# Constants as PE filler, later loads of x8-15, and half an output tile behind the state matrix M

## The chip, the cores and the metric

One core of one Trainium2 chip. The metric is the device time of one execution in microseconds; "span" is what the profile of one execution shows on the core, about 1.7 to 2 us less than that time. The engines are named as in the profile: PE multiplies matrices, PEld loads its weights, DVE, ACT and POOL compute on vectors, SP issues DMAs. The "pitch" is the time from the start of one matmul to the start of the next. "The clock opens" means that the pitch of matmuls with 128 columns falls from 107 to 56 ns; where a time is given for it, it is the start of the trace's first clock record, which the printed views do not show. All runs here carry the state "fast".

## The reference

A layernorm `xn` of x (2048 tokens, 640 features) feeds two branches, and the output is the sum of x and both:

```
xn = layernorm(x)
A: q,k,v = xn @ wqkv (32 heads of 20); phi(t) = where(t > 0, t + 1, exp(t)) + 1e-6
   num = phi(q) @ (phi(k)^T v);  den = phi(q) . sum_s phi(k) + 1e-6;  A = (num / den) @ wo
B: gelu(xn @ w1 + b1) @ w2 + b2          (hidden size 1536)
out = x + A + B
```

Only the start (layernorm, first matmuls with W1) and the join of both branches (the state matrix M, the denominators, the product with W2) matter here.

## The kernel before

x is cut into 16 tiles of 128 tokens. Every tile is normalised on DVE with help of POOL. Tiles 0 to 2 are transposed by PE, tiles 3 to 15 by DMA, issued from SP in order with the loads. A planner turns declared reads and writes of "resources" into semaphore waits; a wait that an earlier instruction of the same engine implied already is left out.

The head, with matmuls on zeros ("filler") that keep PE busy while x arrives, and the loads:

```python
dma_x(0, 1); dma_x(1, 1); dma_w1(0); dma_w1(1); dma_x(2, 1); dma_x(3, 1)   # one line each
dma_w1(2); dma_x(4, 2); dma_w1(3); dma_x(6, 2); dma_x(8, 4)
Pl.ins(v, lambda e: e.memset(warm[:].bitcast(FP32), 0.0), writes=[r_warm])
# ... (cut)
def filler(n):
    b = take(1)
    Pl.ins(pe, [lambda e: e.matmul(bank(b), warm[:, 0:P], warm[:], start=True, stop=True)
                for _ in range(n)], reads=[r_warm], writes=[B_[b]])
def ln_half(t, h):
    s = t % 4
    Pl.ins(v, lambda e: e.bn_stats(stats[:, s, 6*h:6*h+6], x_in[:, t, h*HW:(h+1)*HW]),
           reads=r_x[t], writes=[r_stats[s]])          # one resource for both halves
def ln_aggr(t):
    s = t % 4
    if t < 2:
        Pl.ins(v, lambda e: e.tensor_single_scalar(stats[:, s, 2:3], stats[:, s, 2:3], D * EPS, ALU.add), ...)
    Pl.ins(v, lambda e: e.bn_aggr(aggr[:, s, :], stats[:, s, :]), ...)
    # ... (cut) from tile 2 on POOL adds eps; then POOL: rstd = var ** -0.5
filler(9)
ln_half(0, 0); ln_half(0, 1); ln_aggr(0); ln_half(1, 0); ln_half(1, 1); ln_norm(0)
# ... (cut) transposes of tile 0, b1, filler(1), tile 1
def ln_rest():
    for t in range(4, NT):
        if t + 1 < NT:
            ln_half(t + 1, 0); ln_half(t + 1, 1)       # statistics of t+1 stand before
        ln_norm(t)                                     # the normalisation of t
        if t + 1 < NT: ln_aggr(t + 1)
        xnT_dma(t)                                     # DMA transpose of tile t
        if t == 7: dma_x(12, 4)
```

PE then runs h = W1^T xn^T for tiles 0 to 3 one by one, (4,5), (6,7), (8 to 11), (12 to 15). Much later:

```python
out_mm(0, 0, JT, b0, HALF[:1], [b0])          # W2, tile 0, first half of the columns
den_mm(b0 + 1)                                # denominators, into bank b0+1
m_step([0, 1, DT-1, 2, 3], ahead[1:] + ahead[1:3], lambda: den_eps(b0 + 1))  # M; den_eps after the 2nd
den_rec(); ...; scale_pq(0)
out_mm(0, 0, JT, b0, HALF[1:], [b0 + 1])      # W2, tile 0, second half: wants bank b0+1
for t in range(1, 4):
    out_mm(t, 0, JT, ahead[t], HALF, [ahead[t], ahead[t] + 1])
```

Of the kernel before, what the change touches and what calls it, by code (L numbers as in the profile page):

```python
# [5 lines left out]
ALU = AluOpType  # L6
ACT = mybir.ActivationFunctionType
P = 128
FP32 = mybir.dt.float32
BF16 = mybir.dt.bfloat16  # L10
# [102 lines left out]
def bass_parallel_sum__linear_attn_block__dense_activation_gelu__prompt_kernel(  # L113
    nc: bass.Bass, A_x, A_wqkv, A_wo, B_x, B_w1, B_b1, B_w2, B_b2, out):
    Batch, S, D = A_x.shape
# [7 lines left out]
    JT = F // P  # L123
# [11 lines left out]
    EPS = 1e-5  # L135

    Pl = Planner(nc)
    R_ = Pl.res

    with contextlib.ExitStack() as es:  # L140
        sb = lambda *a, **k: es.enter_context(nc.sbuf_tensor(*a, **k))
# [25 lines left out]
        b1c = sb("b1c", [P, JT], FP32)  # L167
        b2bc = sb("b2bc", [P, D], BF16)
        ident = sb("ident", [P, P], BF16)
        onesm = sb("onesm", [P, P], BF16)  # L170
        hmask = sb("hmask", [P, 3, H], BF16)
        maskKV = sb("maskKV", [P, 2, WD], BF16)
        ZB = sb("ZB", [P, DT, H], BF16)
        warm = sb("warm", [P, 512], BF16)
        stats = sb("stats", [P, 4, 12], FP32)
        aggr = sb("aggr", [P, 4, 2], FP32)
        veps = sb("veps", [P, 4], FP32)
# [10 lines left out]
        B_ = [R_("bank%d" % i) for i in range(8)]  # L188
        ring = [0]

        def take(n):
            b = ring[0]
            if n == 2 and b % 2:
                b += 1
            b %= 8
            ring[0] = (b + n) % 8
            return b

        def bank(b, lo=0, hi=512):
            return ps[:, b * 512 + lo: b * 512 + hi]  # L200
# [4 lines left out]
        def halves(ap):  # L205
            return ap.rearrange("p (a n) -> p a n", a=2)

        r_x = [[R_("x%d" % t)] for t in range(NT)]
# [7 lines left out]
        r_Wq, r_Wv, r_W2 = R_("Wq"), R_("Wv"), R_("W2")  # L216
        r_Wo = [R_("Wo%d" % w) for w in range(NW)]
        r_b1tmp, r_b1c, r_b2 = R_("b1tmp"), R_("b1c"), R_("b2")
        r_ident, r_small, r_ones, r_masks, r_hmask, r_warm = (
            R_("ident"), R_("small"), R_("ones"), R_("masks"), R_("hmask"), R_("warm"))  # L220
        r_stats = [R_("stats%d" % i) for i in range(4)]
        r_aggr = [R_("aggr%d" % i) for i in range(4)]
        r_veps = [R_("veps%d" % i) for i in range(4)]
        r_rstd = [R_("rstd%d" % i) for i in range(NT)]
# [19 lines left out]
        g = "gpsimd"  # L244
        v = "vector"
        s_ = "scalar"
        pe = "tensor"

        def dma(eng, dst, src, writes, reads=()):
            Pl.ins(eng, lambda e: e.dma_start(dst, src), reads=reads, writes=writes, dma=True)  # L250
# [4 lines left out]
        def dma_x(t, n):  # L255
            dma("sync", x_in[:, t:t + n, :], xv[t * P:(t + n) * P, :].rearrange("(t p) d -> p t d", p=P),
                sum(r_x[t:t + n], []))

        def dma_w1(i):
# [10 lines left out]
        dma_x(4, 2)  # L270
        dma_w1(3)
        dma_x(6, 2)
        dma_x(8, 4)

        Pl.ins(v, lambda e: e.memset(warm[:].bitcast(FP32), 0.0), writes=[r_warm])
        Pl.ins(g, lambda e: e.memset(onesm[:], 1.0), writes=[r_ones])
        Pl.ins(g, lambda e: e.memset(mhalf[:], -0.5), writes=[r_small])
        Pl.ins(g, lambda e: e.memset(ident[:], 0.0), writes=[r_ident])
# [3 lines left out]
               reads=[r_ident], writes=[r_ident])  # L282
# [19 lines left out]
            for _ in range(min(n, len(mask_jobs))):  # L302
                mask_jobs.pop(0)()

        def filler(n):
            b = take(1)
            Pl.ins(pe, [lambda e: e.matmul(bank(b), warm[:, 0:P], warm[:], start=True, stop=True)
                        for _ in range(n)], reads=[r_warm], writes=[B_[b]])

        def b1_step():  # L310
            b = take(1)
# [21 lines left out]
        def ln_half(t, h):  # L333
            s = t % 4
            Pl.ins(v, lambda e: e.bn_stats(stats[:, s, 6 * h:6 * h + 6], x_in[:, t, h * HW:(h + 1) * HW]),  # L335
                   reads=r_x[t], writes=[r_stats[s]])

        def ln_aggr(t):
            s = t % 4
            if t < 2:  # L340
                Pl.ins(v, lambda e: e.tensor_single_scalar(stats[:, s, 2:3], stats[:, s, 2:3], D * EPS, ALU.add),
                       reads=[r_stats[s]], writes=[r_stats[s]])
            Pl.ins(v, lambda e: e.bn_aggr(aggr[:, s, :], stats[:, s, :]),
                   reads=[r_stats[s]], writes=[r_aggr[s]])
            if t < 2:
                var, r_var = aggr[:, s, 1:2], r_aggr[s]
            else:
                var, r_var = veps[:, s:s + 1], r_veps[s]
                Pl.ins(g, lambda e: e.tensor_single_scalar(var, aggr[:, s, 1:2], EPS, ALU.add),
                       reads=[r_aggr[s]], writes=[r_var])  # L350
            Pl.ins(g, lambda e: e.tensor_tensor(out=rstd[:, t:t + 1], in0=var, in1=mhalf[:], op=ALU.pow),
                   reads=[r_var, r_small], writes=[r_rstd[t]])
# [30 lines left out]
        def xnT_dma(t):  # L383
            dma_t("sync", xnT[:, :, t * P:(t + 1) * P], xn_tm[:, t, :], r_xnT[t], reads=r_xn[t])

        def h_unit(t0, n, jb):
# [8 lines left out]
                HG[:, jb, tok], bank(b, 0, w), ACT.Gelu_apprx_tanh, bias=b1c[:, jb:jb + 1]),  # L395
                reads=[B_[b], r_b1c], writes=[r_HG[t][jb] for t in range(t0, t0 + n)])

        Pl.ins(s_, lambda e: e.activation(b1c[:, 0:1], warm[:, 0:1], ACT.Gelu_apprx_tanh),
               reads=[r_warm], writes=[r_b1c])

        dma(s_, b1tmp[:], B_b1.rearrange("(a p) -> a p", p=P), [r_b1tmp])
        filler(9)
        ln_half(0, 0)
        ln_half(0, 1)
        ln_aggr(0)
# [3 lines left out]
        b = take(2)  # L409
        transp2(0, b, b + 1)  # L410
        ln_aggr(1)
        copy2(0, b, b + 1)
        b1_step()
        filler(1)
        ln_norm(1)

        h_list = lambda t, n, lo, hi: [(t, n, jb) for jb in range(lo, hi)]
# [6 lines left out]
# [3 lines that stand above are left out]
                    ln_half(t + 1, 0)  # L427
                    ln_half(t + 1, 1)
                ln_norm(t)
                if t + 1 < NT:  # L430
                    ln_aggr(t + 1)
                xnT_dma(t)
                if t == 7:
                    dma_x(12, 4)

        for u in plan:
            if u == "T1":
                b = take(2)
# [8 lines left out]
            elif u == "T2":  # L447
                b = transp(2)
# [36 lines left out]
        for t in range(NT):  # L485
            b = take(2)
# [20 lines left out]
        for k in range(DT):  # L507
            for i in range(DT):
                Pl.ins(g, lambda e, k=k, i=i: e.tensor_copy(plain(Wqkv[:, k, D:2 * D], i), parts(Wqkv[:, k, 0:D], i)),  # L509
                       reads=[r_Wq], writes=[r_Wk, r_WqP])  # L510
# [87 lines left out]
        def m_step(js, bs, after):  # L598
            for n, (j, b) in enumerate(zip(js, bs)):
                for h in range(2):  # L600
                    fns, reads = [], []
                    for a in range(2 if j == DT - 1 else 1):
                        for q in range(4):
                            if j == DT - 1:
                                w, i, last = 2 * q + a, 2, a == 1
                            else:
                                w, i, last = 4 * (j // 2) + q, j % 2, True
                            lhsT = KVP[i][:, w, :]
                            reads += [r_KVP[i], r_Wo[w]]
                            fns.append(lambda e, lhsT=lhsT, w=w, q=q, h=h, b=b, a=a, last=last: e.matmul(  # L610
                                bank(b + h, 0, HW)[32 * q:32 * q + 32, :], lhsT, Wo[:, w, h * HW:(h + 1) * HW],
                                start=(a == 0), stop=last))
                    Pl.ins(pe, fns, reads=reads, writes=[B_[b + h]])
                    m_copy(j, b, h)
                if n == 1:
                    after()

        def den_mm(b):
# [13 lines left out]
        def scale_pq(c):  # L632
            cc = slice(c * CW, (c + 1) * CW)
            for r, (lo, n) in enumerate(((0, 2), (2, 2), (4, 1))):
                Pl.ins(v, lambda e, r=r, lo=lo, n=n: e.tensor_tensor(
                    out=PQ[:, lo:lo + n, cc], in0=PQ[:, lo:lo + n, cc],
                    in1=rsp[:, c, r:r + 1, :].broadcast_to((P, n, CW)), op=ALU.mult),
                    reads=[r_rsp[c][r]] + r_PQ[c][lo:lo + n], writes=r_PQ[c][lo:lo + n])
# [26 lines left out]
        ahead = [(b0 + 2 * i) % 8 for i in range(4)]  # L665

        def out_mm(t, lo, hi, b, w0, w1):
            tok = slice(t * P, (t + 1) * P)
            seq = [(HG[:, jb, tok], W2[:, jb, :], [r_HG[t][jb], r_W2]) for jb in range(JT)]
            seq += [(PQ[:, j, tok], Msb[:, j, :], [r_PQ[t // CH][j]] + r_M[j]) for j in range(DT)]  # L670
            n = len(seq)
            for i in range(lo, hi):
                Pl.ins(pe, [(lambda e, i=i, x=x, bb=bb: e.matmul(  # L673
                    bank(bb, 0, x[1] - x[0]), seq[i][0], seq[i][1][:, x[0]:x[1]],
                    start=(i == 0), stop=(i == n - 1))) for x, bb in zip(w0, w1)],
                    reads=seq[i][2], writes=[B_[bb] for bb in w1], mark=(i in (JT - 1, n - 1)))

        NS = JT + DT
        HALF = [(0, HW), (HW, D)]
# [13 lines left out]
        for c in range(NC):  # L693
            spread(c)
        scale_pq(0)
        out_mm(0, 0, JT, b0, HALF[1:], [b0 + 1])
        for t in range(1, 4):
            b = ahead[t]
            out_mm(t, 0, JT, b, HALF, [b, b + 1])
        for t, b in enumerate(ahead):  # L700
            xb(t)
            out_mm(t, JT, NS, b, HALF, [b, b + 1])
            out_done(t, b)
            if t == 1:
                scale_pq(1)
        for t in range(4, NT - 1):
            b = ahead[t % 4]
# [5 lines left out]
        t = NT - 1  # L713
# [3 lines left out]
        for i, (lo, hi) in enumerate([(0, 320), (320, 512), (512, 640)]):  # L717
            b = take(1)
            r_o = R_("ol%d" % i)
            out_mm(t, 0, NS, b, [(lo, hi)], [b])  # L720
            s = t % 2
            Pl.ins(v, lambda e, lo=lo, hi=hi, b=b: e.tensor_tensor(  # L722
                out=out_sb[:, s, lo:hi], in0=bank(b, 0, hi - lo), in1=x_res[:, t, lo:hi], op=ALU.add),
                reads=[B_[b], r_xb[t]], writes=[r_o] + ([r_out[s]] if i == 0 else []))
# [40 lines left out]
```

## Time and profile before

| | before |
|---|---|
| time, median of 3 | 208.29 us |
| span of the profiled run | 206.39 us |
| first matmul of h | 6.92 us |
| from there to the last matmul group of M | 124.01 us |
| that group to the next matmul | 0.54 us |
| last matmul's end to end of span | 2.45 us |

The rows below the span are start times from the trace and differences of them.

The page of the kernel before, busy time of each engine and the chain of waits:

```profile
PE 201.6 (98%) x1599; PEld 137.6 (67%) x1605; DVE 111.5 (54%) x230; ACT 73.6 (36%) x148; POOL 33.9 (16%) x83
...
PE 95%; DVE 2%; DMA 1%; issue 1%; ACT 0%
```

PE is the bound; a gain has to come from the few places where it idles. Its head, from the timeline of before (start, duration, engine, line, operation, and in brackets the idle time before it):

```profile
1.26 4.02 PE L307 MATMUL ps<-warm 128*128 128x512 bf16 x9 [1.26 <-DVE warm L275]
...
4.17 0.15 DVE L341 TENSOR_SCALAR stats<-stats 128x1 f32<-128x1 f32 x1
...
5.79 0.66 PE L322 MATMUL ps<-ident,xn_tm 128*128 128x128 bf16 x5 [0.51 <-DVE xn_tm L363]
...
6.92 1.00 PE L390 MATMUL ps<-xnT,W 128*128 128x128 bf16 x15
```

The stall after M, from the timeline of before. The addition to the denominators (den_sb) must read its bank before PE may write the second half of tile 0 there:

```profile
130.72 0.68 DVE L626 TENSOR_SCALAR den_sb<-ps 128x512 f32<-128x512 f32 x1
...
131.46 0.31 PE L673 MATMUL ps<-W,HG 128*128 128x320 bf16 x1 [0.24 <-DVE den_sb L626]
```

### The profile page before, as it was taken

The numbers are of one execution on the slowest core, as the hardware profiler recorded it, in microseconds if no ns is written. First come the engines' busy times: TensorE is split into PE (matmuls) and PEld (weight loads), VectorE is DVE, ScalarE is ACT, GpSimd is POOL, SyncE is SP. The second block draws the span as 40 slices with busy tenths as digits, with TensorE's granted clock in tenths as the row PEclk, the third lists the DMA queues.
The fourth block names the chain that finished last, engine by engine and source line by source line (L and its number), as shares of the span: only waits on it lengthen the run. The fifth ranks groups of instructions, "written<-read, shape, count | busy, mean of one in ns | idle before, by whom it ended". The sixth has DMA issues, their size and how long they took to land.

```text
span 206.4 us, 3983 instructions
## 1 busy us (share of the span) xinstructions
PE 201.6 (98%) x1599; PEld 137.6 (67%) x1605; DVE 111.5 (54%) x230; ACT 73.6 (36%) x148; POOL 33.9 (16%) x83
## 2 busy tenths in 40 slices
PE   7899999999999999999999999999999999999995
PEld 2799987444457777777746445677777777777774
DVE  4798674000007888999358888833954322523322
ACT  2699887666676555111153554300000000000000
POOL 2245436400000001999000200000000000000000
PEclk9999999999999999999999999999999999999999
DMA  5996675899500000000000001978611010001011
GB/s 144 350 296 109 168 121 118 272 320 376 188 0 0 3 0 0 3 0 0 0 3 0 2 3 22 370 170 170 150 67 63 32 34 33 32 33 35 32 47 52
DMA packets 24827, 19.70 MB, mean 95 GB/s; under 512 B 9960, under 2 KB 24808, under 8 KB 24808
## 3 DMA queue, kind: packets, MB, share of 16 engines
q1 hardware_dynamic: 23056, 17.86, 29.9%
q10 hardware_dynamic: 1752, 1.58, 4.1%
q8 instruction: 13, 0.21, 0.5%
q14 instruction: 6, 0.05, 0.1%
HBM read 13.11 MB, written 2.62 MB: 76 GB/s over the span
## 4 chain that ended last, share of the span: by engine, by line
PE 95%; DVE 2%; DMA 1%; issue 1%; ACT 0%
PE ps L673 36%; PE ps L390 25%; PE ps L515 11%; PE ps L490 11%; PE ps L556 10%; DMA xPK<-in_A_x_dram 1%; DVE stats L335 1%; PE ps L566 1%; PE ps L620 1%; DVE Msb L595 0%; PE ps L322 0%; DVE den_sb L626 0%; PE ps L610 0%; DVE W L722 0%; DVE xn_tm L363 0%
## 5 line engine op out<-in xcount | busy, mean ns | idle before, releaser
L673 PE MATMUL ps<-W,HG 128*128 128x320 bf16 (+2 forms) x396 | 54.8, 295 | 0.2 <-DVE den_sb L626 0.2
L390 PE MATMUL ps<-xnT,W 128*128 128x128 bf16 (+2 forms) x477 | 52.7, 272 | 0.2
L673 PEld LDWEIGHTS ps<-W,HG 128*128 128x128 bf16 x396 | 38.1, 98 | 14.8 <-DVE den_sb L626 0.5
L390 PEld LDWEIGHTS ps<-xnT,W 128*128 128x128 bf16 x480 | 36.9, 98 | 15.6 <-issue 0.3
L394 ACT ACTIVATE HG<-ps,b1c 128x128 bf16<-128x128 f32 (+2 forms) x96 | 41.5, 475 | 12.1 <-PE ps L390 10.5
L684 DVE TENSOR_TENSOR W<-ps,xnT 128x640 bf16<-128x640 f32 x15 | 12.4, 825 | 35.8 <-PE ps L673 35.4
L478 ACT ACTIVATE ek<-ps 128x512 bf16<-128x512 f32 (+1 forms) x36 | 23.2, 645 | 20.4 <-PE ps L556 10.7
L479 DVE TENSOR_SCALAR ek<-ek 128x512 bf16<-128x512 bf16 (+1 forms) x36 | 11.0, 304 | 35.0 <-ACT ek L478 33.8
L673 PE MATMUL ps<-Msb,PQ 128*128 128x320 bf16 (+2 forms) x165 | 24.2, 295 | 0.0
L490 PE MATMUL ps<-Wqkv,xnT 128*128 128x320 bf16 x160 | 21.9, 299 | 0.0
L515 PE MATMUL ps<-xPK,xn_tm 128*128 128x320 bf16 x160 | 21.9, 299 | 0.0
L556 PE MATMUL ps<-xnT,Wqkv 128*128 128x512 bf16 x97 | 21.4, 379 | 0.2
L673 PEld LDWEIGHTS ps<-Msb,PQ 128*128 128x128 bf16 x165 | 15.9, 98 | 5.9
L490 PEld LDWEIGHTS ps<-Wqkv,xnT 128*128 128x128 bf16 x160 | 15.7, 98 | 6.2
L515 PEld LDWEIGHTS ps<-xPK,xn_tm 128*128 128x128 bf16 x160 | 15.7, 98 | 6.1
L509 POOL COPY Wqkv<-Wqkv 128x128 bf16<-128x128 bf16 x25 | 15.1, 603 | 22.9 <-PE ps L490 21.4
L335 DVE BATCH_NORM_STATS2 stats<-xPK 128x6 f32<-128x320 bf16 x32 | 15.2, 474 | 4.6 <-DMA xPK<-in_A_x_dram 4.1
L556 PEld LDWEIGHTS ps<-xnT,Wqkv 128*128 128x128 bf16 x100 | 9.7, 98 | 11.4
L481 DVE SCALAR_TENSOR_TENSOR PQ<-ps,ek 128x512 bf16<-128x512 f32 x20 | 13.8, 691 | 2.1
L481 DVE SCALAR_TENSOR_TENSOR xPK<-ps,ek 128x640 bf16<-128x640 f32 x16 | 13.2, 824 | 1.7
L527 DVE TENSOR_TENSOR Msb<-Msb,xPK 128x640 f32<-128x640 f32 x14 | 11.6, 825 | 0.5
L519 ACT ACTIVATE W<-ps 128x640 bf16<-128x640 f32 x5 | 3.5, 704 | 18.2 <-PE ps L515 18.2
(60 smaller groups left out, 82.6 us busy)
## 6 DMA issues: line engine op xcount, KB each, us to landing
xnT<-in_A_x_dram SPq DMA_DIRECT2D x4, 640.0 KB, 6.2
Wqkv<-in_A_wqkv_dram SPq DMA_DIRECT2D x3, 800.0 KB, 6.9
out_dram<-W SPq DMA_DIRECT2D x15, 160.0 KB, 1.8
W<-in_B_w_dram SPq DMA_DIRECT2D x4, 480.0 KB, 6.1
W<-in_B_w_dram SPq DMA_DIRECT2D x1, 1920.0 KB, 14.5
xn_tm<-rden ACTq DMA_DIRECT2D x12, 128.0 KB, 3.4
xPK<-in_A_x_dram SPq DMA_DIRECT2D x2, 640.0 KB, 7.2
Wo<-in_A_wo_dram SPq DMA_DIRECT2D x8, 160.0 KB, 8.4
```

The source lines that it names most:

```text
L335: Pl.ins(v, lambda e: e.bn_stats(stats[:, s, 6 * h:6 * h + 6], x_in[:, t, h * HW:(h + 1) * HW]), reads=r_x[t], writes=[r_stats[s]])
L390: Pl.ins(pe, [(lambda e, k=k: e.matmul(bank(b, 0, w), W1[:, k, jb * P:(jb + 1) * P], xnT[:, k, tok], start=(k == 0), stop=(k == DT - 1))) ...
L394: Pl.ins(s_, lambda e: e.activation(HG[:, jb, tok], bank(b, 0, w), ACT.Gelu_apprx_tanh, bias=b1c[:, jb:jb + 1]), reads=[B_[b], r_b1c], wri ...
L478: Pl.ins(s_, lambda e: e.activation(e2, src, ACT.Exp), reads=br, writes=[r_ek[s]])
L481: Pl.ins(v, lambda e: e.scalar_tensor_tensor(out=d2, in0=src, scalar=0.0, in1=e2, op0=ALU.max, op1=ALU.add), reads=br + [r_ek[s]], writes= ...
L490: fns.append(lambda e, k=k, h=h, b=b, t=t: e.matmul(bank(b + h, 0, HW), xnT[:, k, t * P:(t + 1) * P], Wqkv[:, k, D + h * HW:D + (h + 1) * ...
L509: Pl.ins(g, lambda e, k=k, i=i: e.tensor_copy(plain(Wqkv[:, k, D:2 * D], i), parts(Wqkv[:, k, 0:D], i)), reads=[r_Wq], writes=[r_Wk, r_WqP])
L515: Pl.ins(pe, [(lambda e, t=t, h=h, b=b, f=f, i=i: e.matmul(bank(b + h, 0, HW), xn_tm[:, t, f * P:(f + 1) * P], PK[:, t, h * HW:(h + 1) * H ...
L527: Pl.ins(v, lambda e, t=t: e.tensor_tensor(out=zsum, in0=zsum, in1=PK[:, t, :], op=ALU.add), reads=[r_PK[t], r_zsum], writes=[r_zsum])
L556: Pl.ins(pe, [(lambda e, k=k, j=j, b=b: e.matmul(bank(b), Wqkv[:, k, D + j * P:D + (j + 1) * P], xnT[:, k, cc], start=(k == 0), stop=(k == ...
L673: Pl.ins(pe, [(lambda e, i=i, x=x, bb=bb: e.matmul(bank(bb, 0, x[1] - x[0]), seq[i][0], seq[i][1][:, x[0]:x[1]], start=(i == 0), stop=(i = ...
L684: Pl.ins(v, lambda e: e.tensor_tensor(out=halves(out_sb[:, s, :]), in0=pair(b), in1=halves(x_res[:, t, :]), op=ALU.add), reads=B_[b:b + 2] ...
```

## The change

Its intent: keep PE busy from its first moment, so that its clock rises early; take the small addition off DVE's path in the head; keep the DMA transposes of tiles 3 to 5 clear of the big load of x8-11 in front of them; fill the stall after M.

```diff
-        dma_x(8, 4)
-        Pl.ins(v, lambda e: e.memset(warm[:].bitcast(FP32), 0.0), writes=[r_warm])
+        def filler(n, w=512):
+            Pl.ins(pe, [lambda e: e.matmul(bank(b, 0, w), nc.const_aps.tensor(1.0, [P, P], BF16),
+                                           nc.const_aps.tensor(1.0, [P, w], BF16), ...) ...], writes=[B_[b]])
-        r_stats = [R_("stats%d" % i) for i in range(4)]
+        r_stats = [[R_("stats%d_%d" % (i, h)) for h in range(2)] for i in range(4)]
@@ ln_half
-                   reads=r_x[t], writes=[r_stats[s]])
+                   reads=r_x[t], writes=[r_stats[s][h]])
+            if t < 2 and h == 0:
+                Pl.ins(g, lambda e: e.tensor_single_scalar(stats[:, s, 2:3], ..., D * EPS, ALU.add), ...)
@@ ln_aggr: the addition on DVE goes; reads=r_stats[s] (both halves)
@@ head
-        filler(9)
+        filler(10)
+        filler(6, P)
-        filler(1)
+        filler(3, P)
@@ ln_rest
-                if t == 7:
+                if t == 5:
+                    dma_x(8, 4)
                     dma_x(12, 4)
@@ m_step
-                if n == 1:
+                if n == 2:
                     after()
@@ after M
         scale_pq(0)
+        out_mm(3, 0, JT, ahead[3], HALF[:1], [ahead[3]])
         out_mm(0, 0, JT, b0, HALF[1:], [b0 + 1])
-        for t in range(1, 4):
+        for t in range(1, 3):
             ...
+        out_mm(3, 0, JT, ahead[3], HALF[1:], [ahead[3] + 1])
```

(Cut. ACT's first activation also reads a constant instead of `warm`, so it no longer waits for DVE.)

More of the change, by code (lines that the diff above doesn't have):

```diff
@@ L173, in bass_parallel_sum__linear_attn_block__dense_activation_gelu__prompt_kernel @@
         ZB = sb("ZB", [P, DT, H], BF16)
-        warm = sb("warm", [P, 512], BF16)
         stats = sb("stats", [P, 4, 12], FP32)
@@ L218, in bass_parallel_sum__linear_attn_block__dense_activation_gelu__prompt_kernel @@
         r_b1tmp, r_b1c, r_b2 = R_("b1tmp"), R_("b1c"), R_("b2")
-        r_ident, r_small, r_ones, r_masks, r_hmask, r_warm = (
-            R_("ident"), R_("small"), R_("ones"), R_("masks"), R_("hmask"), R_("warm"))
-        r_stats = [R_("stats%d" % i) for i in range(4)]
+        r_ident, r_small, r_ones, r_masks, r_hmask = (
+            R_("ident"), R_("small"), R_("ones"), R_("masks"), R_("hmask"))
+        r_stats = [[R_("stats%d_%d" % (i, h)) for h in range(2)] for i in range(4)]
         r_aggr = [R_("aggr%d" % i) for i in range(4)]
@@ L303, in run_masks @@
                 mask_jobs.pop(0)()
-        def filler(n):
+        def filler(n, w=512):
             b = take(1)
-            Pl.ins(pe, [lambda e: e.matmul(bank(b), warm[:, 0:P], warm[:], start=True, stop=True)
-                        for _ in range(n)], reads=[r_warm], writes=[B_[b]])
+            Pl.ins(pe, [lambda e: e.matmul(bank(b, 0, w), nc.const_aps.tensor(1.0, [P, P], BF16),
+                                           nc.const_aps.tensor(1.0, [P, w], BF16), start=True, stop=True)
+                        for _ in range(n)], writes=[B_[b]])
         def b1_step():
@@ L335, in ln_half @@
             Pl.ins(v, lambda e: e.bn_stats(stats[:, s, 6 * h:6 * h + 6], x_in[:, t, h * HW:(h + 1) * HW]),
-                   reads=r_x[t], writes=[r_stats[s]])
+                   reads=r_x[t], writes=[r_stats[s][h]])
+            if t < 2 and h == 0:
+                Pl.ins(g, lambda e: e.tensor_single_scalar(stats[:, s, 2:3], stats[:, s, 2:3], D * EPS, ALU.add),
+                       reads=[r_stats[s][0]], writes=[r_stats[s][0]])
         def ln_aggr(t):
             s = t % 4
-            if t < 2:
-                Pl.ins(v, lambda e: e.tensor_single_scalar(stats[:, s, 2:3], stats[:, s, 2:3], D * EPS, ALU.add),
-                       reads=[r_stats[s]], writes=[r_stats[s]])
             Pl.ins(v, lambda e: e.bn_aggr(aggr[:, s, :], stats[:, s, :]),
-                   reads=[r_stats[s]], writes=[r_aggr[s]])
+                   reads=r_stats[s], writes=[r_aggr[s]])
             if t < 2:
@@ L396, in h_unit @@
                 reads=[B_[b], r_b1c], writes=[r_HG[t][jb] for t in range(t0, t0 + n)])
-        Pl.ins(s_, lambda e: e.activation(b1c[:, 0:1], warm[:, 0:1], ACT.Gelu_apprx_tanh),
-               reads=[r_warm], writes=[r_b1c])
+        Pl.ins(s_, lambda e: e.activation(b1c[:, 0:1], nc.const_aps.tensor(0.0, [P, 1], FP32), ACT.Gelu_apprx_tanh),
+               writes=[r_b1c])
         dma(s_, b1tmp[:], B_b1.rearrange("(a p) -> a p", p=P), [r_b1tmp])
-        filler(9)
+        filler(10)
+        filler(6, P)
         ln_half(0, 0)
```

## The prediction

> **What bounds the kernel now.** PE. The page gives PE 201.6 us busy of 206.4; the chain of waits is PE for 95%. From the first real matmul (6.92 us, timeline) to the last (203.9) PE is busy but for a few 0.05 us pauses and one stall. A change gains only before 6.92, in that stall, or in the last 2.4 us, which it leaves alone. No real PE work is removed.
>
> **The stall (on the path).** The last matmul group of M starts at 130.91; at the pitch of 0.136 us the next matmul was due at 131.05 and starts at 131.46, released by the addition that empties the denominator bank (DVE den_sb, 130.72 to 131.40): 0.41 us. The change puts 12 matmuls of tile 3 there (12 x 0.136 = 1.63 us). ACT emptied their bank at 130.90, so they start at once. The addition moves behind one more Msb copy and ends near 131.8; its bank is now wanted at 132.7. Gain 0.41 us, whole. Scaled PQ is ready at about 141.4 and PE comes for it at about 142.4 instead of 142.88: no new wait.
>
> **The head (mostly not on the path).** Before: x tile 0 lands 3.09, statistics, a 0.17 us addition on DVE, aggregate, normalise, transposes at 5.79, copies, h at 6.92. The addition goes to POOL (about 0.22 us, beside the second statistics, 0.51 us): normalised data comes 0.19 us earlier, about 5.60. But:
> - The fillers (10 of 512, 6 of 128 columns) start at about 0.9 instead of 1.26; cold pitches in this trace are 0.427 and 0.107 us, so they end at 0.9 + 4.27 + 0.64 = 5.8, after 5.60. That eats the 0.19 unless the clock is up earlier. The Trainium skill, "TensorE: Matmul & The Clock Gate", Part 1, says the clock doubles after about 3.4 us of activity in a free-running window; this trace agrees roughly: transposes from 5.79 at 107 ns pitch, h matmuls at 56 ns. With the same window phase nothing is gained; with another, up to 0.3 us.
> - The weights cap it: W1's second quarter lands at 7.91 and is wanted at 8.03, so the head is worth 0.1 us at most. Tile 2's transposes (11.38; data normalised at 11.15) cap it near 0.15.
> I book 0.03 us.
>
> **x8-15 later.** Before, x8-11 lands at 16.76 and tile 3's DMA transpose behind it at 17.27, while PE wants tile 3 at 17.52: no stall. After, tile 3 should land by 15.5 and tile 5 by 19.3 (before 20.57, wanted 20.9): slack, not time. The price: x8-11, issued at about 17.7, lands at about 21.5 to 22.5; DVE waits about 2 us for it at the statistics of tile 8, which stand before tile 7's normalisation. Estimate: tile 7 lands at 25.5 to 26.5 (wanted 27.3), tile 11 at 32 to 33 (wanted 33.9). The wait for x12-15 (2.19 us at 24.35) disappears. I expect no PE stall; this is the main risk.
>
> **Predicted:** 208.29 - 0.41 - 0.03 = 207.85 us; 8 in 10 between 207.40 and 208.25. Faster by over 2%: 0.01; within 2%: 0.98; slower: 0.01.
>
> **What would show it.** PE stall at den_sb gone, tile 3's 12 matmuls following M at 0.136 us. First filler near 0.9, no PE idle before the transposes; transposes at 5.6 to 5.9; h at 6.8 to 7.0. DVE's long DMA wait near 19.5 instead of 24.35. No PE gap at 17.4, 20.8, 27.3 or 33.9.
>
> **What would make it wrong.** A clock window that opens earlier or later; W1 landing before 7.9 (more head gain); x8-11 slow behind the transposes, so that PE waits for tile 7 or 11 (up to 1 us lost).

## More of the kernel before

The cadence of the normalisation loop, DVE alone, timeline of before: 1.56 us from tile to tile.

```profile
14.42 0.45 DVE L363 TENSOR_SCALAR xn_tm<-xPK,aggr,rstd 128x640 bf16<-128x640 bf16 x1
14.78 0.20 DVE L343 BATCH_NORM_AGGREGATE aggr<-stats 128x2 f32<-128x12 f32 x1
14.90 0.97 DVE L335 BATCH_NORM_STATS2 stats<-xPK 128x6 f32<-128x320 bf16 x2
15.98 0.45 DVE L363 TENSOR_SCALAR xn_tm<-xPK,aggr,rstd 128x640 bf16<-128x640 bf16 x1
```

And the waits of DVE in before (total us, times, longest):

```profile
DVE stats L335 <- DMA xPK<-in_A_x_dram: 4.1, 2, 2.2
...
DVE xn_tm L363 <- POOL rstd L351: 0.3, 1, 0.3
```

## The result, and the profile after

The changed kernel took 208.39 us (median of 6, 207.95 to 208.65); before, in all its runs up to then, 208.37 (median of 6, 208.16 to 208.89). The ratio is 0.9992, 95% interval 0.9975 to 1.0009. Ratios here are the mean time of one kernel's fast runs over the mean of the other's fast runs of the same rounds, so they are not quite the ratios of the medians. So: no difference that can be told from noise. 0.9992 of 208.29 is 208.12, inside the predicted range, which is wide enough to hold almost the whole way from the forecast to "no change"; the raw median 208.39 lies 0.14 above its upper end, as the median of before rose too. A gain of 0.44 was expected and did not appear.

The page after:

```profile
PE 202.7 (98%) x1614; PEld 138.0 (67%) x1614; DVE 109.6 (53%) x227; ACT 73.6 (36%) x148; POOL 34.5 (17%) x85
...
PE 85%; DMA 5%; DVE 3%; POOL 3%; issue 2%; SPq 0%; ACT 0%; DVEq 0%
```

The chain of waits has left PE: 15% of it now runs elsewhere, over DMA, DVE and POOL above all. In time order it goes through the following pieces (start, length, what; those between the first two are the normalisation loop):

```profile
17.74 5.83 DMA xPK<-in_A_x_dram
...
31.75 2.64 DMA xnT<-xn_tm
34.39 0.34 issue
34.73 26.06 PE ps L388 x120
```

x8-11 is under way from 17.74 to 23.57. From there the normalisation loop runs to tile 11, whose transpose lands at 34.39; PE starts on tiles 8 to 11 at 34.73. The 0.34 us between contains two instructions of PE's sequencer that only wait. The waits of after say the same:

```profile
DVE stats L333 <- DMA xPK<-in_A_x_dram: 8.6, 2, 5.4
...
DVE xn_tm L361 <- POOL rstd L349: 3.7, 12, 0.3
...
PE ps L388 <- DMA xnT<-xn_tm: 0.5, 1, 0.5
```

DVE's longest wait for x grew from 2.2 to 5.4 us, and a wait for POOL now stands in front of 12 normalisations (before: 1). The loop has become slower, DVE timeline of after:

```profile
14.39 0.45 DVE L361 TENSOR_SCALAR xn_tm<-xPK,aggr,rstd 128x640 bf16<-128x640 bf16 x1 [0.32 <-POOL rstd L349]
14.75 0.20 DVE L341 BATCH_NORM_AGGREGATE aggr<-stats 128x2 f32<-128x12 f32 x1
14.87 0.83 DVE L333 BATCH_NORM_STATS2 stats<-xPK 128x6 f32<-128x320 bf16 x2
16.02 0.45 DVE L361 TENSOR_SCALAR xn_tm<-xPK,aggr,rstd 128x640 bf16<-128x640 bf16 x1 [0.32 <-POOL rstd L349]
```

1.63 us from tile to tile instead of 1.56, although the statistics themselves take less (0.83 against 0.97). The stall after M has shrunk, timeline of after:

```profile
131.26 0.72 PE L610 MATMUL ps<-Wo,W 128*32 128x320 bf16 x16
...
131.89 0.68 DVE L626 TENSOR_SCALAR den_sb<-ps 128x512 f32<-128x512 f32 x1
131.90 0.79 PEld L673 LDWEIGHTS ps<-W,HG 128*128 128x128 bf16 x7 [0.19 <-ACT Msb L592]
131.91 0.99 PE L673 MATMUL ps<-W,HG 128*128 128x320 bf16 x6
```

PE no longer waits for den_sb. What is left, 0.231 us from start to start instead of the pitch of 0.136, the profile puts down to ACT's copy that empties the bank of tile 3's half. That does not fit: the copy's signal comes at 131.66, and the weight load starts 0.24 us later, while in before it started 0.04 us after den_sb's signal. PE also changes here from matmuls on 32 columns of its array (128*32) to matmuls on all 128 (128*128). At the opposite change, from W2 to the denominators, the step is 0.229 to 0.230 us in all 14 profiles, though the signal waited for there had come 0.59 us earlier. So the 0.095 us go with the change of form; no run separates it. The head:

```profile
0.85 4.58 PE L304 MATMUL ps<-const-bfloat16-1.0 128*128 128x512 bf16 x16 [0.85 <-PEq L752]
...
5.73 0.54 PE L320 MATMUL ps<-ident,xn_tm 128*128 128x128 bf16 x5 [0.30 <-DVE xn_tm L361]
...
6.74 1.00 PE L388 MATMUL ps<-xnT,W 128*128 128x128 bf16 x15
```

The account of the two profiled runs, which closes on the spans' difference of +0.31 us:

| term | before | after | difference |
|---|---|---|---|
| first matmul of h | 6.917 | 6.742 | -0.175 |
| waits between h and M (stretch minus 124.01) | 0.00 | 0.93 | +0.93 |
| last group of M to next matmul | 0.538 | 0.231 | -0.307 |
| last matmul's end to end of span | 2.452 | 2.316 | -0.136 |

The last row belongs to no edit that is known: over all profiles it lies between 2.29 and 2.52, and e7, which has only the head of the change, has 2.31. The 0.93 splits, by what the matmul starts exceed their pitch, into 0.12 at tile 5 (20.8), 0.17 at tile 7 (27.5) and 0.65 at tile 11 (34.7).

**Theory A:** the later load of x8-11 makes tiles 7 and 11 late, and this eats the gains of head and middle. **Rival B:** it is the split of the statistics' resource, which lengthens the loop by 0.07 us a tile. **Rival C:** head and middle gain nothing in the first place.

### The profile page after: what moved, and what is told of

Read it like the earlier page. It is cut to its first block, busy times and chain, and to the rows that moved or that the text cites. A ratio compares the mean times of both kernels' runs of the same rounds, so it can differ in the third digit from the quotient of the medians.

```text
span 206.7 us, 4035 instructions
## 1 busy us (share of the span) xinstructions
PE 202.7 (98%) x1614; PEld 138.0 (67%) x1614; DVE 109.6 (53%) x227; ACT 73.6 (36%) x148; POOL 34.5 (17%) x85
## 4 chain that ended last, share of the span: by engine, by line
PE 85%; DMA 5%; DVE 3%; POOL 3%; issue 2%; SPq 0%; ACT 0%; DVEq 0%
PE ps L673 36%; PE ps L388 15%; PE ps L490 11%; PE ps L515 11%; PE ps L556 10%; DMA xPK<-in_A_x_dram 4%; POOL rstd L349 2%; DVE stats L333 1%; DMA xnT<-xn_tm 1%; DVE aggr L341 1%; PE ps L610 1%; DVE xn_tm L361 1%; PE ps L566 1%; POOL veps L347 1%; PE ps L620 1%
## 5 line engine op out<-in xcount | busy, mean ns | idle before, releaser
L388 PE MATMUL ps<-xnT,W 128*128 128x128 bf16 (+2 forms) x480 | 53.3, 272 | 0.6 <-DMA xnT<-xn_tm 0.5
L556 PE MATMUL ps<-xnT,Wqkv 128*128 128x512 bf16 x100 | 21.9, 379 | 0.0
L509 POOL COPY Wqkv<-Wqkv 128x128 bf16<-128x128 bf16 x25 | 15.1, 603 | 22.9 <-PE ps L490 21.4
L333 DVE BATCH_NORM_STATS2 stats<-xPK 128x6 f32<-128x320 bf16 x32 | 13.7, 467 | 8.7 <-DMA xPK<-in_A_x_dram 8.6
```

Of the source, the lines that this page charges most:

```text
L333: Pl.ins(v, lambda e: e.bn_stats(stats[:, s, 6 * h:6 * h + 6], x_in[:, t, h * HW:(h + 1) * HW]), reads=r_x[t], writes=[r_stats[s][h]])
L388: Pl.ins(pe, [(lambda e, k=k: e.matmul(bank(b, 0, w), W1[:, k, jb * P:(jb + 1) * P], xnT[:, k, tok], start=(k == 0), stop=(k == DT - 1))) ...
L509: Pl.ins(g, lambda e, k=k, i=i: e.tensor_copy(plain(Wqkv[:, k, D:2 * D], i), parts(Wqkv[:, k, 0:D], i)), reads=[r_Wq], writes=[r_Wk, r_WqP])
L556: Pl.ins(pe, [(lambda e, k=k, j=j, b=b: e.matmul(bank(b), Wqkv[:, k, D + j * P:D + (j + 1) * P], xnT[:, k, cc], start=(k == 0), stop=(k == ...
```

## The experiments

Twelve runs, all correct; f1 and f4 repeat the kernels before and after. "Waits" is the stretch from the first h matmul to the last group of M, minus 124.01 us, in the profiled run. In f3 the 1.72 is no wait: it is the slow pitch of the matmuls up to 10.4 us.

| run | first h | waits | M to next | span | times (median; lowest to highest) |
|---|---|---|---|---|---|
| e1_w2_only | 6.801 | 0.00 | 0.231 | 205.83 | 207.96; 207.56 to 209.52 |
| e2_x_only | 6.617 | 2.42 | 0.539 | 208.51 | 208.81; 208.09 to 210.24 |
| e3_x_undone | 6.683 | 0.68 | 0.232 | 206.39 | 208.13; 207.62 to 208.24 |
| e4_split_t01 | 6.672 | 0.00 | 0.232 | 205.71 | 207.83; 207.53 to 208.72 |
| e5_x_later | 6.618 | 2.23 | 0.232 | 207.88 | 209.56; 209.40 to 209.82 |
| e6_x_pieces | 6.631 | 0.04 | 0.232 | 205.68 | 207.65; 207.40 to 207.89 |
| e7_head_only | 6.587 | 0.62 | 0.536 | 206.54 | 208.34; 208.04 to 208.80 |
| e8_b1_late | 6.916 | 0.70 | 0.232 | 206.65 | 208.05; 207.95 to 208.38 |
| f1_before_again | 6.912 | 0.39 | 0.537 | 206.84 | 209.17; 208.09 to 209.97 |
| f2_before_fill11 | 6.782 | 0.74 | 0.536 | 207.00 | 208.42; 207.76 to 208.83 |
| f3_gap | 6.795 | 1.72 | 0.232 | 207.65 | 209.71; 209.01 to 210.79 |
| f4_after_again | 6.918 | 0.29 | 0.231 | 206.23 | 208.17; 207.67 to 208.66 |

Before was timed beside each group of four: 208.27 (207.87 to 210.22) beside e1 to e4, 208.62 (207.89 to 210.21) beside e5 to e8, 208.28 (207.94 to 208.65) beside f1 to f4, 11 runs each.

### e1_w2_only: the middle alone

```diff
 # before, plus only:
-                if n == 1:
+                if n == 2:
+        out_mm(3, 0, JT, ahead[3], HALF[:1], [ahead[3]])     # and the other half behind tile 2
```

> Before, with only the half of tile 3 behind M (and the denominator addition one Msb copy later). Theory A (this part gains and the rest of the change takes it back): the 0.40 us stall at the denominator bank shrinks to about 0.10 us, the pause seen in the changed kernel between M and tile 3's half (131.68 to 131.91); time 0.3 us below before, ratio 0.9985. Rival C (the gain of this part does not reach the end): ratio 1.000.

Measured: the pause after M is 0.231 instead of 0.538 us and no waits appear elsewhere. The median is 0.31 below before's, but two of six runs lie over 209, so the ratio 0.9981 (0.9932 to 1.0031) decides nothing. The gain of 0.31 us is shown by the profile, where it reaches the end; the clock times allow it and do not prove it.

### e2_x_only: the later loads alone

```diff
-        dma_x(8, 4)
-                if t == 7:
+                if t == 5:
+                    dma_x(8, 4)
```

> Before, with only the later loads of x8-15. Theory A (the later loads alone starve PE): x8-11 lands near 23.6, tile 11's transpose near 34.4, PE waits for it 0.4 to 0.7 us at about 34; ratio 1.002 to 1.003. Rival B (the split of the statistics into two resources is what makes tile 11 late, 0.075 us a tile): statistics cadence 1.56 us a tile as before, tile 11 lands at about 34.0, PE waits under 0.2 us there; ratio at most 1.001.

Measured: ratio 1.0012 (0.9964 to 1.0060), times from 208.09 to 210.24. The profile fell on the slowest, and there the damage is larger than either theory said: x8-11 landed only at 25.12, and tile 7 came 2.25 us late. The DVE and PE timelines of e2_x_only:

```profile
25.14 1.02 DVE L334 BATCH_NORM_STATS2 stats<-xPK 128x6 f32<-128x320 bf16 x2 [7.34 <-DMA xPK<-in_A_x_dram]
```

```profile
29.49 7.85 PE L389 MATMUL ps<-xnT,W 128*128 128x256 bf16 x65 [2.08 <-issue]
```

(The PE line names "issue" as what ended its wait, but the transpose of tile 7 landed at 29.40.) With the cadence at 1.56 us, the wait is there, so B alone does not explain what later loads can do; but this profile shows the slowest of six runs, not a typical one. How late x8-11 lands varies: 4.9 us after issue in e5, 5.3 to 5.8 in after, e4, e8 and f4, 7.7 here.

Why so long? Here are windows of after (columns: stretch, busy time of each engine, clock, DMA share, GB/s), and last one window of e5_x_later, in which x8-11 is issued only at 20.02:

```profile
16.00:17.00 1.00, 1.00 (x22) 1.00 (x19) 0.98 (x4) 1.00 (x5) 0.24 (x2) 1.00 0.82 164
...
18.50:19.50 1.00, 1.00 (x22) 1.00 (x20) 0.00 (x0) 1.00 (x4) 0.60 (x2) 1.00 0.04 4
19.50:20.50 1.00, 1.00 (x22) 1.00 (x20) 0.00 (x0) 1.00 (x5) 0.00 (x0) 1.00 0.74 73
...
21.50:22.50 1.00, 1.00 (x12) 0.90 (x10) 0.00 (x0) 0.87 (x2) 0.00 (x0) 1.00 1.09 381
```

```profile
18.50:19.50 1.00, 1.00 (x21) 1.00 (x19) 0.00 (x0) 1.00 (x5) 0.62 (x2) 1.00 0.13 6
```

In after, where the load follows tile 5's transpose on the queue, almost nothing moves for two microseconds (4 and 73 GB/s); then come 163 and 381 GB/s. It is tempting to blame the turn from transpose to load, but the first of these two microseconds is as empty in e5 (6 GB/s), before the load is issued, and in e7 (8 GB/s), with no load of x near. Tile 5's transpose takes 4.05 to 4.72 us from issue to landing in all 14 profiles, tile 4's 2.56 to 3.06. So tile 5's transpose is slow with or without a load of x behind it, and a load placed behind it starts late. The load's own start is slow as well: from its first packets, near 20.1, it takes about a microsecond to come to speed. The load of x12-15, issued 1.8 us behind, may have its part too, since by 22.75 the packets of both add up to the size of x8-11, which landed at 23.57; this is an estimate from the packets of that trace, and no run separates it. Before has such a pause too, where tile 3's transpose meets the load of x8-11, and there it hurts nobody:

```profile
12.00:13.00 1.00, 1.00 (x22) 1.00 (x19) 1.00 (x3) 0.86 (x4) 0.22 (x1) 1.00 1.08 360
...
15.50:16.50 1.00, 1.00 (x22) 1.00 (x19) 0.89 (x4) 1.00 (x5) 0.44 (x1) 1.00 0.10 13
```

The Trainium skill, "DMA: Bandwidth & Descriptors", section "Rules for kernel authors", says that a transpose next to ordinary DMAs needs nothing. The context there is correctness, and all runs here were correct; in time, these traces show pauses of 1 to 2 us in such a row, not only at the turn. What causes them, no run here shows.

### e3_x_undone: the change without the later loads

> The changed kernel with x8-11 and x12-15 loaded where they were before. Theory A: no PE wait over 0.1 us between 7 and 60 us, since tile 3 lands at about 17.3 and is wanted at about 17.35; span about 0.5 us under before; ratio to before 0.9975. Rival (the later loads were needed: with PE earlier, tile 3 arrives too late): a PE wait of 0.1 to 0.3 us near 17.4 and ratio 0.998 to 0.999. If rival C holds (head and middle gain nothing): ratio 1.000.

Measured: 208.13, ratio 0.9966 (0.9925 to 1.0006). The waits did not vanish: 0.68 us. 0.20 at 8.0 is W1's second quarter (landed 7.95), 0.11 at tile 3 (landed 17.57), 0.35 at tile 5 (landed 21.23; PE was ready for it at 20.98). So with PE earlier, tiles 3 and 5 become the next limit. Undoing the later loads took away the waits for tiles 7 and 11 (0.81) and left 0.66 elsewhere. The rival here was right about tile 3; no expectation had named tile 5 as a limit. Its slack is thin even without the change: f1, the unchanged kernel, waits 0.39 us for it (landed 21.17), while in before it landed at 20.57 and cost nothing.

### e4_split_t01: the change with one statistics resource from tile 2 on

```diff
-                   reads=r_x[t], writes=[r_stats[s][h]])
+                   reads=r_x[t], writes=[r_stats[s][h]] if t < 2 else r_stats[s])
```

> The changed kernel, but from tile 2 on the two statistics of a tile share one resource again, as before. Theory B (the split costs one extra wait instruction, about 0.07 us, in front of every normalisation): cadence of the normalisations back from 1.635 to 1.56 us, tile 11 lands about 0.3 to 0.5 us earlier than 34.39, PE's wait at 34 falls from 0.65 to about 0.2 to 0.35; ratio to before about 0.998. If only the loads matter: cadence 1.635 or the wait at 34 stays at 0.6 or more, ratio 0.9995.

Measured: 207.83, ratio 0.9967 (0.9920 to 1.0014), and the waits are gone altogether (0.00), more than Theory B had expected. DVE timeline of e4_split_t01, 1.56 us from tile to tile again:

```profile
14.17 0.45 DVE L361 TENSOR_SCALAR xn_tm<-xPK,aggr,rstd 128x640 bf16<-128x640 bf16 x1
...
15.73 0.45 DVE L361 TENSOR_SCALAR xn_tm<-xPK,aggr,rstd 128x640 bf16<-128x640 bf16 x1
```

So the split does cost the 0.07 us a tile. The trace shows how. Before, the second half's statistics waited for the first half's, since both wrote one resource; that wait implied that the previous tile's aggregate was done, and the normalisation had one semaphore to wait for, POOL's. With the split the second wait is no longer implied. The trace then has a separate waiting instruction on DVE in front of each normalisation: POOL's result ends at 15.915, the waiting instruction runs from 15.952 to 15.973, the normalisation starts at 16.022. Before: 15.941, then 15.977. 0.107 against 0.036 us, on the one chain that sets the loop's pace (aggregate, POOL twice, normalise). In the chain of waits of after it stands as "DVEq":

```profile
25.34 0.58 POOL rstd L349
25.92 0.03 issue
25.94 0.02 DVEq L94
25.96 0.05 issue
26.01 0.46 DVE xn_tm L361
```

How much of the 0.93 is the split's? Tile 11 landed 0.95 us earlier than in after (33.44 against 34.39). 0.47 of it lies in the loop between the normalisations of tile 7 and tile 11 (6.22 against 6.69 us; besides the 0.07 us a tile, the step from tile 8 to 9 takes 1.78 to 1.80 us in all six profiles with the split and 1.56 without it, where no load is awaited), though not all of that reached the landing, since the transposes queue up behind one another; 0.29 is the earlier issue of x8-11 (17.45 against 17.74), of which 0.22 again is the shorter loop up to tile 5; 0.49 is that x8-11 took 5.34 instead of 5.83 us, which the edit does not explain. So e4 shows that the cadence is the split's and that without it the later loads can just be met; the exact share of the 0.93 stays open, because the loads vary.

### e5_x_later: one transpose later still

```diff
-                if t == 5:
+                if t == 6:
                     dma_x(8, 4)
```

> The changed kernel with x8-15 issued one transpose later still, behind tile 6 instead of tile 5. Theory A: each 0.1 us that x8-11 is later is 0.1 us more PE wait at tile 11; issue about 1.6 to 2 us later, x8-11 lands near 25.2, PE waits for tiles 7 and 11 together 2 to 2.6 us instead of 0.8; ratio to before about 1.007 to 1.009. Rival (the wait at 34 has another cause): ratio stays at 1.000 to 1.002.

Measured: 209.56, 1.2 to 1.4 us above the medians of the changed kernel (208.39 and 208.17), waits 2.23. Tiles 7 and 11 account for 1.79 of it (1.32 and 0.47), less than the 2 to 2.6 that A expected for these two; the rest is 0.34 at tile 5 and 0.09 at W1. x8-11 landed at 24.92, 1.35 us later than in after, and the waits for the two tiles grew by 0.98, not at tile 11, as A had it, but at tile 7. The ratio to before, 1.0041 (0.9996 to 1.0086), is lower than expected because three of before's 11 runs beside it were over 209. The dose works in sum: later loads, later tiles, though by less than one for one.

### e6_x_pieces: a version that keeps the gains

```diff
 # after, with e4's one resource from tile 2 on, and:
         dma_x(6, 2)
+        dma_x(8, 2)
                 if t == 5:
-                    dma_x(8, 4)
-                    dma_x(12, 4)
+                    dma_x(10, 2)
+                if t == 7:
+                    dma_x(12, 4)
```

> The changed kernel with one resource for the statistics from tile 2 on, and x in pieces: x8-9 in front, x10-11 behind tile 5's transpose, x12-15 behind tile 7's as before. Theory A and B: tile 3 lands near 15.8 to 16.5, no PE wait over 0.1 us from 7 to 60; head 0.17 and middle 0.3 remain, span about 0.5 us under before, ratio 0.9975. Rival C: ratio 1.000 though the waits are gone.

Measured: 207.65 (207.40 to 207.89), ratio to before 0.9948 (0.9917 to 0.9979), the only experiment under before whose interval excludes 1. Tile 3 landed at 16.54, tile 5 at 20.48, tile 11 at 30.86; waits 0.04. The span is 0.71 under before's: 0.29 head, 0.31 middle, 0.16 at the end, less 0.04 of waits. It is the fastest kernel. Tile 11 now lands 2.87 us before PE starts on it; in e4, also without waits, it was 0.28. Part of the ratio is before's three runs over 209, and an interval that excludes 1 is weaker than it looks: f1, the unchanged kernel against itself, gave 1.0043 (1.0018 to 1.0068). What counts more is that all six runs of e6 lie at or below 207.89, and all 39 of before at or above 207.87. Against before's median on the other chips (208.27, 208.28) the gain is 0.6 us, 0.3%. It was not run beside the changed kernel on one chip.

### e7_head_only: the head alone

> Before, with only the head of the change: constants as filler, the addition on GpSimd, the split statistics. Theory: first h matmul 0.1 to 0.2 us earlier, capped by W1's second quarter (lands 7.8 to 7.9); cadence 1.635; denominator stall still 0.4; ratio 0.9990 to 0.9997. Rival: the head gives nothing or costs (fillers push the transposes out when the clock opens late): ratio 1.000 or more.

Measured: 208.34, ratio 0.9983 (0.9951 to 1.0014). The first h matmul starts at 6.587, earlier than in any other run, and 0.62 us are lost again: 0.25 at 7.95, where W1's second quarter landed at 7.90 (the cap named in the prediction), and 0.37 at tile 5 (landed 21.08). In this profile the head alone gave 0.33 us and lost more.

### e8_b1_late: does the earlier b1 load hold up x1?

In after, x1 landed at 4.48 instead of 3.67 and held up the statistics; the b1 load had moved to between x0's and x1's issue.

```diff
+               reads=[r_ident], writes=[r_b1c])      # ACT's first activation, before the b1 load
```

> The changed kernel, but ACT's first activation waits for the identity matrix again, so that the b1 load is issued at about 1.75 instead of 0.89, behind x1's issue. Theory D (the b1 load, now issued between x0's and x1's, pushes x1's landing from 3.67 to 4.48 and so delays the statistics of tile 1 and the first normalisation by about 0.15): x1 lands at about 3.7, the first transpose starts at about 5.6 instead of 5.73. Rival: x1 lands anywhere from 3.6 to 4.5 from run to run, whatever the b1 load does. Time within 0.1 us of the changed kernel either way, since W1's second quarter caps the head.

Measured: x1 landed at 3.50, but it landed at 3.55 to 3.62 also in e3 to e7, f3 and f4, where the b1 load is as early as in after. Theory D falls: 4.48 was one execution's accident. The first h matmul came late, at 6.916, because this run's clock opened late, at 6.79: fillers and transposes ran at the slow pitch, and the transposes could not start before 5.70, as in f4.

### f1_before_again, f2_before_fill11, f3_gap, f4_after_again: the clock, and the runs over 209

By now the kernels with the old filler had shown runs over 209 us, and those with the new filler none but e5, whose loads explain it. Theory E supposes that PE's idle half microsecond in front of the transposes sometimes makes the clock open late. The text for f1 counts 10 of 40; recounted it was 11.

```diff
 # f2: before, with                      # f3: e6_x_pieces, with
-        filler(9)                        -        filler(10)
+        filler(11)                       -        filler(6, P)
                                          +        filler(5)
                                          +        filler(1, P)
```

> The kernel before once more, for another look with a profile and six more times. The kernels with the old filler (before and the two experiments built on it) showed times over 209 in 10 of their 40 runs so far, about 1.5 to 2 us above their others; the kernels with the new filler in none of 34 (x8-15 one transpose later left out). Theory E (the clock: with the old filler PE idles about 0.5 us in front of the first transposes[...]): one to three of the six runs over 209, and if the profiled one is among them its matmuls run at the slow pitch past 7 us. Rival F (the loads: one of the pauses between DMA transposes and plain loads is sometimes longer): such a run shows a PE wait for xnT or W1 instead, and the pitch is fast from 7 us on.

> The kernel before with 11 fillers of 512 columns instead of 9, so that the 0.5 us of idle PE in front of the transposes is closed, while all else (start at 1.26, b1 load, loads of x) stays. Theory E: no run over 209 (old filler: about one in four); median as the fast runs of before, plus up to 0.35 where the clock opens late and the fillers push the transposes out. Rival F: still one or two of six over 209.

> The kernel of e6_x_pieces with 5 fillers of 512 and one of 128 columns in front of the transposes instead of 10 and 6, so that PE idles about 2.5 us there. Theory E: the clock opens near 8 to 10 us in most runs, the first 60 to 150 h matmuls run at 107 ns instead of 56; time 0.6 to 2 us above e6_x_pieces' 207.65, and spread widely. If the clock needs no such filling (rival F): time within 0.2 us of e6_x_pieces.

> The changed kernel once more beside before, on the same chip as the three others. Theory E: no run over 209; PE waits for tiles 5, 7 and 11 sum to 0.5 to 1 us as in the first profile; median near 208.3, before's fast runs near 208.2 and some of its runs over 209, so ratio 0.996 to 1.000.

f3 shows what a gap in front of the transposes costs: 209.71 (ratio to before 1.0084, 1.0059 to 1.0110) against 207.65 of e6_x_pieces, which ran on another chip (spans 207.65 and 205.68). Timelines of PE, f3_gap first, then e6_x_pieces:

```profile
0.84 2.40 PE L305 MATMUL ps<-const-bfloat16-1.0 128*128 128x512 bf16 x6 [0.84 <-PEq L754]
5.61 0.71 PE L321 MATMUL ps<-ident,xn_tm 128*128 128x128 bf16 x5 [2.36 <-DVE xn_tm L362]
...
6.79 1.76 PE L389 MATMUL ps<-xnT,W 128*128 128x128 bf16 x15
```

```profile
6.63 1.00 PE L389 MATMUL ps<-xnT,W 128*128 128x128 bf16 x15
```

The 15 h matmuls take 1.76 instead of 1.00 us, and the slow pitch (107 ns) lasts to 10.4 us, over some 30 h matmuls instead of the 60 to 150 expected. The windows of the two show it too, and a trap with it (f3_gap, then e6_x_pieces):

```profile
8.00:9.00 1.00, 1.00 (x13) 1.00 (x11) 0.00 (x0) 0.78 (x3) 0.00 (x0) 1.00 1.11 334
```

```profile
8.00:9.00 1.00, 1.00 (x22) 1.00 (x19) 0.96 (x3) 1.00 (x5) 0.00 (x0) 1.00 1.05 343
```

PE is 100% busy in both and the clock column reads 1.00 in both; only the count of matmuls, 13 against 22, tells the slow clock.

f4, the changed kernel again: 208.17, ratio 0.9997 (0.9984 to 1.0010), no run over 209, waits 0.29, all at tile 11, less than the 0.5 to 1 expected. Its clock opened at 6.42, and its head is worth nothing: the transposes follow the fillers directly at 5.70, at the slow pitch, and h starts at 6.92 as in before.

```profile
5.70 0.74 PE L320 MATMUL ps<-ident,xn_tm 128*128 128x128 bf16 x5
...
6.92 1.00 PE L388 MATMUL ps<-xnT,W 128*128 128x128 bf16 x15
```

f1 and f2 leave the runs over 209 open. f1, the unchanged kernel, had three of six over 209, while the very same kernel beside it, on the same chip, had none of 11 (ratio 1.0043, 1.0018 to 1.0068, for one and the same kernel). Its profile fell on a run of 208.56 and shows a clock open at 6.16 and a wait of 0.39 us for tile 5. f2, gap closed, took 208.42 (ratio 1.0004, 0.9988 to 1.0020) and had none of six over 209, which theory E expects, but so had before. Counted over all: old filler 14 of 57 runs over 209 (before 6 of 39, e1 2, e2 3, f1 3 of 6 each); new filler, f3 and e5 left out, 0 of 40; f2 0 of 6. The one such run with a profile is e2's, 210.24: there the clock opened at 5.33 and the loss was a late load (rival F). A clock that opens as late as in f3 (10.44) would cost as much, but no profiled run of before shows it. Whether the new filler removes these runs, or they only come in clusters, is not settled.

## Why the prediction was right or wrong

- **The total.** "208.29 - 0.41 - 0.03 = 207.85" missed; the ratio puts the changed kernel at 208.1. That this lies in the range is owed to the range's width, not to the account: two terms gained, and one that was booked as zero took most of it back (in the profiled run more than all of it).
- **"I expect no PE stall" (x8-15 later).** Wrong, and the step that failed. Waits of 0.93 us in the first profile, 0.29 in the second. The mechanism stood in the prediction as the main risk; the sizes of three terms were off. x8-11, issued when predicted, landed at 23.57, not "21.5 to 22.5": it stood behind tile 5's slow transpose and came to speed slowly. Before's own trace gave a warning: x12-15, of the same size and placed behind tile 7's transpose, took 5.17 us from issue to landing (21.34 to 26.52), which would have put x8-11 at 22.9. Tile 11 landed at 34.39, not "32 to 33": besides the later load, the loop ran at 1.63 instead of 1.56 us a tile. And "wanted 33.9" took no account of the 0.34 us between landing and first matmul once PE has to wait.
- **The split of the statistics' resource.** Not in the prediction at all. It looked like bookkeeping for the head and touches every tile: one more waiting instruction in front of 12 normalisations, and, through the later issue, a later x8-11. e4 shows it.
- **"Gain 0.41 us, whole" (the stall).** Right mechanism, size 0.31. PE started tile 3's half 0.095 us behind the pitch. The bank was free in time, as predicted (131.66; the next matmul was due at 131.81). What the prediction left out is the change from matmuls on 32 columns to matmuls on 128: the opposite change costs the same 0.093 us above the pitch in every profile. The Trainium skill, "TensorE: Matmul & The Clock Gate", says in its table that the queue pulls weight loads ahead of running matmuls; here that holds within a row of equal matmuls, where a load starts 0.13 us before its matmul, but at these two changes the first load starts only 1 to 4 ns before it. No run separates this further.
- **The head.** "With the same window phase nothing is gained; with another, up to 0.3 us": right. With the clock opening after 6 us, h starts at 6.91 to 6.92 with the old filler (before, f1) and with the new (f4, e8); with an earlier opening, at 6.59 to 6.80 (f3, whose few fillers cannot hold up the transposes, left out). But e1 and e2, with the old head, reach 6.80 and 6.62 as well, so an early first h matmul alone is not the change's doing. Counted from the landing of tile 0, the path to h takes 3.72 us with the old head and an early clock (e1, e2, f2) and 3.44 to 3.45 with the new (e3 to e7; 3.55 in after, where x1 came late): the new head is worth 0.27 us, if the clock opens early. With a late clock its fillers end at 5.70 and take this away. The clock opens at different times in two runs of one kernel (by 4.9 us in after, as the pitch shows, at 6.42 in f4), and no run shows what sets this, so what the head gains in one run is luck. The cap by W1's second quarter is shown by e3 and e7 (0.20 and 0.25 us lost at about 7.95). Tile 5's transpose, a second cap in e3 and e7, was only seen as slack.
- **Theories.** C is false for the middle: 0.31 in every profile that has the edit. A and B both hold: A by e5 (dose) and e2, B by the cadence in e4. Neither alone gives the 0.93, and its exact division is open.

## What to carry to other kernels

When a change makes the bounding engine earlier, list for every input how long before its use it lands; the smallest slack is what the gain is worth, and moving a load to protect one input must be checked against all inputs behind it. A big load in a row of DMA transposes can start late behind a slow one, and took 4.9 to 7.7 us to land here, so read from the trace how long such a load takes in that place, cut it into pieces if need be, and place each piece where its consumer has slack. Finer dependency tracking is not free: a split that removes one implied wait can put an additional waiting instruction into a loop, so look at the cadence of every loop that uses the resource.

## What the Trainium skill lacked or had wrong

- "DMA: Bandwidth & Descriptors", "Rules for kernel authors": nothing on pauses in a row of DMA transposes and plain loads on one queue. Here 4 GB/s for 1 us and 73 GB/s for the next, after 145 and before 163 and 381 GB/s; tile 5's transpose took 4.05 to 4.72 us in every profile where tile 4's took 2.56 to 3.06, and a load of 640 KB behind it or behind tile 6's took 4.9 to 7.7 us from issue to landing.
- "TensorE: Matmul & The Clock Gate", Part 1: it puts the change of pitch at around 4 us of sustained matmuls, give or take 0.5 us, after a busy window of about 3.4 us. Here, with filler from 0.84 us on, the clock opened between 3.49 (e3) and 6.79 (e8), so 2.6 to 5.9 us after the first matmul. Both ends lie outside 4 plus or minus 0.5. 2.6 is also less than a full window; either a partly busy window was enough there, or PE had been active before the span, which the trace does not show.
- No page that I looked through says that an instruction with a second semaphore to wait for can cost an additional instruction: 0.07 us on DVE here.
- "TensorE: Matmul & The Clock Gate", Part 1, does not say that the slow state can be missing from a table of granted clocks: the clock column reads 1.00 at 13 and at 22 matmuls per microsecond, since the clock record of f3 begins only when the clock opens, at 10.44 us.
- "TensorEngine Tiling (Array Packing)", "Key Properties", has no figure for the change between matmuls on 128 and on 32 columns: 0.229 to 0.232 us from start to start here, at a pitch of 0.136.
